# Attention and MLP on one core: q, k, v cast on GpSimd and turned by DMA, A@V in one burst per quad

## The chip, the cores and the metric

The kernel runs on one core of a Trainium2 chip. The metric is device time in microseconds of one execution. Two runs of the kernel before took 523.96 and 526.88 us, median 525.42.

## What is computed

q, k and v are f32 of shape (8, 12, 448, 64): 8 batches, 12 heads, 448 tokens, head size 64. The attention has a squared relu in place of the softmax, and an MLP with prelu follows:

```python
scores = scale * np.matmul(q, k.transpose(0, 1, 3, 2))      # scale = 1/sqrt(64)
attn = np.maximum(scores, 0.0) ** 2 / S                     # S = 448
attn_out = np.matmul(attn, v)
x = attn_out.transpose(0, 2, 1, 3).reshape(B * S, H * D)    # 3584 x 768
h = x @ w_in                                                # 768 x 2048
g = np.maximum(h, 0.0) + alpha * np.minimum(h, 0.0)
out = g @ w_out                                             # 2048 x 768, f32
```

## The kernel before

Four heads make a quad, so a batch has three quads and the program 24. The 448 tokens are split as 64 partitions times 7 (PP and NJ), and a chunk (b, g, j) is one seventh of the keys of one quad.

Loads (`load_batch`, lines 67 to 84): q, k and v of a batch come by DMA from the GpSimd (POOL) queue, which casts f32 to bf16 on the way; q and k in pieces of 64 elements, since heads are interleaved in SBUF. The raw tiles have two buffers, one batch each. w_in comes in 16 transfers (line 92), w_out in one (line 106), on the same queue, between the loads of batches 0 and 1.

`transposes` (line 111): 14 transposes on TensorE turn q and k of a quad, seven each into a PSUM tile `tps` from `mm_ps`, the pool of two banks that the MLP uses too; VectorE copies each to SBUF (qT, kT, line 119).

`scores` (line 121): four 64x64 matmuls into a pair of banks `sc` (two pairs), a relu on ScalarE (line 132) or, for j = 2 and 5, on VectorE (line 134), and a square on VectorE (line 136) give `at`. `attnv` (line 139): four matmuls for each j add up in `av`, one pair of banks with one buffer; after j = 6 ScalarE scales it into xT (line 154).

`ffn1` (line 159): six matmuls into a bank of `mm_ps` (`hps`), relu of the negative on ScalarE (`neg`, line 169), prelu on VectorE into gT (line 170), which frees the bank. `ffn2` (line 175): 16 matmuls into a bank of `mm_ps` (`ops`), copied by ScalarE to `osb` (line 184); two output transfers from the SP queue for each 128 rows.

The order is written by hand, and each engine follows it. The attention of batch 0 runs first. Then batch b's MLP steps (16 of ffn1 with cost 1.12, 6 or 8 of ffn2 with cost 2.6) are mixed with bursts of batch b + 1: a burst is the scores of two chunks and A@V of the two chunks before. A quad's transposes come right after the burst that has chunk j = 2 of the quad ahead of it.

Of the kernel before, what the change touches and what calls it, by code (L numbers as in the profile page):

```python
# [19 lines left out]
PP = 64  # L20
NJ = 7
# [3 lines left out]
def kernel(  # L25
# [32 lines left out]
    ident = singles.tile([128, 128], BF16)  # L58
# [6 lines left out]
    raw = {}  # L65

    def load_batch(b, which, parts):
        src = {"q": q, "k": k, "v": v}[which]
        t = raw.get((b, which))
        if t is None:  # L70
            shape = [128, H // 2, NJ, D] if which == "v" else [128, NG, NJ, 2, D]
            t = raw_pool.tile(shape, BF16, tag=which, name=f"{which}raw")
            raw[(b, which)] = t
        if which == "v":
            flat = src[b].rearrange("(m two) (pp j) d -> (two pp) m (j d)", two=2, j=NJ)
            for lo, hi in parts:
                nc.gpsimd.dma_start(out=t[:, 2 * lo:2 * hi].rearrange("p m j d -> p m (j d)"),  # L77
                                    in_=flat[:, 2 * lo:2 * hi])
        else:
            flat = src[b].rearrange("(m two) (pp j) d -> (two pp) m j d", two=2, j=NJ)  # L80
            for lo, hi in parts:
                for g in range(lo, hi):
                    for s in range(2):
                        nc.gpsimd.dma_start(out=t[:, g, :, s], in_=flat[:, 2 * g + s])  # L84

# [8 lines left out]

    nc.sync.dma_start(out=alpha_sb, in_=moe_alpha.rearrange("(kf p) -> p kf", p=128))
    nc.vector.tensor_scalar(beta_sb, alpha_sb, -1.0, 1.0, ALU.mult, ALU.add)
    make_identity(nc, ident)
    for w in "qkv":
        load_batch(0, w, [(0, 1)])
    for w in "qkv":  # L100
        load_batch(0, w, [(1, 3)])
    for i in range(4):
        load_w_in(512 * i, 512 * i + 512)
    for w in "qkv":
        load_batch(1, w, [(0, 3)])
    nc.gpsimd.dma_start(out=w_out_sb, in_=w_out_v)


    qT, kT, att, av, xT = {}, {}, {}, {}, {}

    def transposes(b, g):
        for name, store, eng in (("q", qT, nc.vector), ("k", kT, nc.vector)):
            ps = mm_ps.tile([128, NJ, 128], BF16, tag="mm", name="tps")
            src = raw[(b, name)]
            for j in range(NJ):
                nc.tensor.transpose(ps[:, j], src[:, g, j].rearrange("p s d -> p (s d)"), ident)  # L116
            dst = qkT_pool.tile([128, 2, NJ, PP], BF16, tag=name, name=f"{name}T")
            store[(b, g)] = dst
            eng.tensor_copy(dst, ps.rearrange("p j (h c) -> p h j c", h=2))  # L119

    def scores(b, g, j):
        ps = sc_ps.tile([128, 2, 512], F32, tag="sc", name="sc")
        qt, kt = qT[(b, g)], kT[(b, g)]
        for r in range(2):
            for c in range(2):
                nc.tensor.matmul(ps[64 * c:64 * c + 64, r, :S],  # L126
                                 kt[64 * r:64 * r + 64, c, j, :],
                                 qt[64 * r:64 * r + 64, c],
                                 start=True, stop=True)
        rl = at_pool.tile([128, 2, S], BF16, tag="rl", name="rl")  # L130
        if j not in (2, 5):
            nc.scalar.activation(rl, ps[:, :, :S], ACTF.Relu)  # L132
        else:
            nc.vector.tensor_scalar(rl, ps[:, :, :S], 0.0, None, ALU.max)  # L134
        a = at_pool.tile([128, 2, S], BF16, tag="at", name="at")
        nc.vector.tensor_tensor(a, rl, rl, ALU.mult)  # L136
        att[(b, g, j)] = a

    def attnv(b, g, j):
        if j == 0:  # L140
            av[(b, g)] = av_ps.tile([128, 2, 512], F32, tag="av", name="av")
        ps = av[(b, g)]
        a = att.pop((b, g, j))
        vv = raw[(b, "v")]
        for r in range(2):
            for s in range(2):
                nc.tensor.matmul(ps[64 * s:64 * s + 64, r, :S],  # L147
                                 vv[64 * r:64 * r + 64, 2 * g + s, j, :],
                                 a[64 * r:64 * r + 64, s],
                                 start=(j == 0), stop=(j == NJ - 1))  # L150
        if j == NJ - 1:
            if g == 0:
                xT[b] = xT_pool.tile([128, NG, 2, S], BF16, tag="xT", name="xT")
            nc.scalar.activation(xT[b][:, g], ps[:, :, :S], ACTF.Copy, scale=out_scale)  # L154


    gT = {}

# [13 lines left out]

    o_sb = {}
# [27 lines left out]

    bursts = {b: [] for b in range(B)}
    pend = []
    for i in range(0, len(chunks), 2):
        new = chunks[i:i + 2]
        bursts[new[0][0]].append((new, pend))
        pend = new
    last_pend = pend

    def emit_burst(new, old):  # L210
        for ch in new:
            scores(*ch)
            if ch[2] == 2:
                n = quads.index(ch[:2]) + 1
                if n < len(quads):
                    todo.append(quads[n])
        for ch in old:
            attnv(*ch)

    todo = []  # L220
    transposes(0, 0)
    for new, old in bursts[0]:
        emit_burst(new, old)
        while todo:
            transposes(*todo.pop(0))
    for b in range(B):
        steps = mlp_steps(b)
        work = bursts[b + 1] if b + 1 < B else []
        total = sum(c for c, _ in steps) * 0.88
        done, n = 0.0, 0  # L230
        if b + 2 < B:
            for w in "qkv":
                load_batch(b + 2, w, [(0, 3)])
        if b == B - 1:
            for ch in last_pend:
                attnv(*ch)
        for cost, fn in steps:
            while n < len(work) and done >= total * n / len(work):
                emit_burst(*work[n])
                n += 1  # L240
                while todo:
                    transposes(*todo.pop(0))
            fn()
            done += cost
        assert n == len(work)

# [29 lines left out]
```

## Time and profile before

| | us |
|---|---|
| median of the two runs | 525.42 |
| profiled execution | 527.37 |
| its span, first to last instruction | 525.6 |
| TensorE busy | 434.0 |
| VectorE busy | 262.0 |
| ScalarE busy | 216.7 |
| GpSimd busy | 112.8 |

The mean granted TensorE clock is 0.936 of full speed. In the tables of waits a row says which line of which engine sat idle until what; in the timeline the bracket at a row's end is the idle time ahead of the row and what ended it. Engines: PE is TensorE, DVE is VectorE, ACT is ScalarE, POOL is GpSimd, SP only issues DMAs. Most of POOL's busy time is the issuing of DMAs.

### The profile page before, as it was taken

Reading aid. Unit: us, or ns where it says so; the run is one execution under the profiler, and the core shown is the slowest. Engines: PE = TensorE matmul, PEld = TensorE weight load, DVE = VectorE, ACT = ScalarE, POOL = GpSimd, SP = SyncE. Lnnn points to the kernel's source line nnn. Section 1 sums busy time; section 2 is a strip of 40 time slices with the busy share of each in tenths; the row PEclk is TensorE's granted clock in tenths of the full one; section 3 lists DMA queues with packets and bytes.
Section 4 is the critical chain, followed back from the end, with each engine's and each line's share of the span. In section 5 each row is a group of like instructions: output and inputs, shape, how many; then the busy total and the mean of one; then the engine's idle time right before and its main releaser. Section 6 shows DMA issues by size and latency. Waiting matters only on the chain.

```text
span 525.6 us, 7922 instructions
## 1 busy us (share of the span) xinstructions
PE 434.0 (83%) x3344; PEld 220.5 (42%) x3344; DVE 262.0 (50%) x393; ACT 216.7 (41%) x329; POOL 112.8 (21%) x128
## 2 busy tenths in 40 slices
PE   2744979888899898898798897897888978989996
PEld 1411434443355443443345443453434533444453
DVE  1855475445653376435755365544655257633500
ACT  1443344443552363353444354534544345343411
POOL 9688066000440008000080004300000000000000
PEclk9775798998999898998999998999989999899998
DMA  9999999160492509423092325914001210012013
GB/s 93 166 187 157 205 141 113 34 110 1 30 106 58 87 0 86 53 62 52 1 104 62 77 38 38 84 46 82 2 1 30 61 31 2 0 31 61 0 43 79
DMA packets 105811, 34.34 MB, mean 65 GB/s; under 512 B 90928, under 2 KB 102192, under 8 KB 105776
## 3 DMA queue, kind: packets, MB, share of 16 engines
q0 software_dynamic: 99232, 22.81, 47.5%
q1 hardware_dynamic: 6544, 11.02, 8.5%
q8 instruction: 26, 0.43, 0.3%
q14 instruction: 9, 0.07, 0.0%
HBM read 45.62 MB, written 11.01 MB: 108 GB/s over the span
## 4 chain that ended last, share of the span: by engine, by line
PE 54%; DVE 20%; ACT 12%; POOL 5%; DMA 5%; issue 4%; ACTq 0%; POOLq 0%
PE ops L178 29%; PE hps L164 20%; DVE at L136 8%; ACT rl L132 7%; DVE rl L134 5%; DVE gT L170 5%; ACT neg L169 4%; DMA vraw<-in_v_dram 3%; PE sc L126 2%; POOL qraw L84 2%; POOL kraw L84 2%; PE av L147 2%; DVE qT L119 2%; DMA w_in_sb<-in_moe_w_in_dram 1%; ACT xT L154 1%
## 5 line engine op out<-in xcount | busy, mean ns | idle before, releaser
L164 PE MATMUL hps<-xT,w_in_sb 128*128 128x448 bf16 x768 | 175.4, 381 | 34.7 <-DVE qT L119 19.9
L178 PE MATMUL ops<-w_out_sb,gT 128*128 128x384 bf16 x896 | 151.5, 326 | 8.5 <-DVE qT L119 6.7
L136 DVE TENSOR_TENSOR at<-rl 128x896 bf16<-128x896 bf16 x168 | 102.6, 624 | 108.1 <-ACT rl L132 103.6
L170 DVE SCALAR_TENSOR_TENSOR gT<-neg,beta_sb,hps 128x448 bf16<-128x448 f32 x128 | 85.6, 678 | 95.6 <-ACT neg L169 95.6
L164 PEld LDWEIGHTS <-w_in_sb 128*128 128x128 bf16 x768 | 77.8, 104 | 127.0 <-issue 75.8
L169 ACT ACTIVATE neg<-hps 128x448 f32<-128x448 f32 x128 | 69.3, 544 | 145.1 <-PE hps L164 145.1
L132 ACT ACTIVATE rl<-sc 128x896 bf16<-128x896 f32 x120 | 106.4, 919 | 31.5 <-PE sc L126 29.7
L178 PEld LDWEIGHTS <-gT 128*128 128x128 bf16 x896 | 85.8, 98 | 72.1 <-issue 18.3
L184 ACT COPY osb<-ops 128x384 f32<-128x384 f32 x56 | 26.8, 478 | 127.0 <-PE ops L178 127.0
L84 POOL DMA_DIRECT2D qraw<-in_q_dram x48 | 46.9, 979 | 103.7 <-PE tps L116 102.7
L147 PE MATMUL av<-at,vraw 64*64 64x448 bf16 x672 | 52.0, 368 | 20.2 <-ACT xT L154 16.7
L134 DVE TENSOR_SCALAR rl<-sc 128x896 bf16<-128x896 f32 x48 | 52.1, 1085 | 14.3 <-PE sc L126 14.3
L126 PE MATMUL sc<-qT,kT 64*64 64x448 bf16 x672 | 52.6, 382 | 4.8 <-ACT rl L132 3.0
L84 POOL DMA_DIRECT2D kraw<-in_k_dram x48 | 46.8, 977 | 15.8 <-DMA w_out_sb<-in_moe_w_out_dram 13.4
L147 PEld LDWEIGHTS <-vraw 64*64 64x64 bf16 x672 | 22.4, 110 | 38.3 <-issue 23.7
L77 POOL DMA_DIRECT2D vraw<-in_v_dram x9 | 7.4, 818 | 119.4 <-PE av L147 119.4
L126 PEld LDWEIGHTS <-kT 64*64 64x64 bf16 x672 | 14.4, 108 | 35.7 <-issue 34.2
L116 PE MATMUL tps<-ident,qraw 128*128 128x128 bf16 x168 | 15.3, 239 | 12.1 <-DMA qraw<-in_q_dram 12.1
L154 ACT ACTIVATE xT<-av 128x896 bf16<-128x896 f32 x24 | 22.3, 929 | 0.0
L116 PE MATMUL tps<-ident,kraw 128*128 128x128 bf16 x168 | 15.2, 238 | 6.1 <-DMA kraw<-in_k_dram 6.1
L119 DVE COPY qT<-tps 128x896 bf16<-128x896 bf16 x24 | 14.8, 618 | 9.8 <-PE tps L116 9.8
L116 PEld LDWEIGHTS <-qraw 128*128 128x128 bf16 x168 | 10.8, 106 | 19.1 <-issue 13.2
(12 smaller groups left out, 41.0 us busy)
## 6 DMA issues: line engine op xcount, KB each, us to landing
out_dram<-osb SPq DMA_DIRECT2D x56, 192.0 KB, 2.7
qraw<-in_q_dram POOLq DMA_DIRECT2D x48, 112.0 KB, 4.1
kraw<-in_k_dram POOLq DMA_DIRECT2D x48, 112.0 KB, 4.4
vraw<-in_v_dram POOLq DMA_DIRECT2D x7, 672.0 KB, 7.4
w_in_sb<-in_moe_w_in_dram POOLq DMA_DIRECT2D x16, 192.0 KB, 7.7
w_out_sb<-in_moe_w_out_dram POOLq DMA_DIRECT2D x1, 3072.0 KB, 23.3
vraw<-in_v_dram POOLq DMA_DIRECT2D x1, 448.0 KB, 7.4
vraw<-in_v_dram POOLq DMA_DIRECT2D x1, 224.0 KB, 5.6
```

Of the source, the lines that this page charges most:

```text
L84: nc.gpsimd.dma_start(out=t[:, g, :, s], in_=flat[:, 2 * g + s])
L116: nc.tensor.transpose(ps[:, j], src[:, g, j].rearrange("p s d -> p (s d)"), ident)
L126: nc.tensor.matmul(ps[64 * c:64 * c + 64, r, :S], kt[64 * r:64 * r + 64, c, j, :], qt[64 * r:64 * r + 64, c], start=True, stop=True)
L132: nc.scalar.activation(rl, ps[:, :, :S], ACTF.Relu)
L134: nc.vector.tensor_scalar(rl, ps[:, :, :S], 0.0, None, ALU.max)
L136: nc.vector.tensor_tensor(a, rl, rl, ALU.mult)
L147: nc.tensor.matmul(ps[64 * s:64 * s + 64, r, :S], vv[64 * r:64 * r + 64, 2 * g + s, j, :], a[64 * r:64 * r + 64, s], start=(j == 0), stop= ...
L154: nc.scalar.activation(xT[b][:, g], ps[:, :, :S], ACTF.Copy, scale=out_scale)
L164: nc.tensor.matmul(ps, w_in_sb[:, km // 2, km % 2, bass.ts(ff, 128)], xT[b][:, km // 2, km % 2, :], start=(km == 0), stop=(km == KM - 1))
L169: nc.scalar.activation(neg, ps, ACTF.Relu, scale=-1.0)
L170: nc.vector.scalar_tensor_tensor(gT[b // 2][:, ff, (b % 2) * S:(b % 2) * S + S], neg, beta_sb[:, ff:ff + 1], ps, ALU.mult, ALU.add)
L178: nc.tensor.matmul(ps, gT[sb][:, ff, bass.ts(c, 128)], w_out_sb[:, ff, bass.ts(hf, 384)], start=(ff == 0), stop=(ff == KF - 1))
```

## The change

Loads: each quad's q, k and v come as plain f32 transfers from the SP queue, one each, with three raw buffers (a quad each), four quads ahead. Three casts then make bf16 tiles, on GpSimd (for quads 0 to 2: k on ScalarE, q on VectorE, v on GpSimd). q and k are turned by one DMA transpose each (SBUF to SBUF, 7 blocks of 128x128) from the SP queue, straight into qT and kT; TensorE's transposes, the identity and the copies on VectorE are gone.

Attention: `attnv` runs a quad's 28 matmuls in one go, in a pair of banks taken from the score pool, after the first scores of the next quad. The pool `av` is gone and `mm_ps` has four banks. All relus are ScalarE's except j = 2 and 5 of quads 0 to 2. The output copy `osb` moves from ScalarE to VectorE. A quad is four bursts (1 + A@V, 2, 2, 2 scores), spread over the MLP steps of the batch before.

Start: the loads of quads 0 to 3 go out on SP, w_in and w_out on POOL ahead of all casts.

```diff
-    sc_ps = ctx.enter_context(tc.tile_pool(name="scps", bufs=2, space=bass.MemoryType.PSUM))
-    av_ps = ctx.enter_context(tc.tile_pool(name="avps", bufs=1, space=bass.MemoryType.PSUM))
-    mm_ps = ctx.enter_context(tc.tile_pool(name="mmps", bufs=2, space=bass.MemoryType.PSUM))
+    sc_ps = pool("scps", 2, **PSUM)
+    mm_ps = pool("mmps", 4, **PSUM)
...
+    def load(n, names="qkv"):
+        b, g = quads[n]
+        for w in names:
+            t = raw_pool.tile([128, 2, NJ, D], F32, tag=w, name=f"{w}raw")
+            raw[(n, w)] = t
+            flat = src[w][b, 4 * g:4 * g + 4].rearrange("(s hf) (pp j) d -> (hf pp) s (j d)", hf=2, j=NJ)
+            nc.sync.dma_start(out=t.rearrange("p s j d -> p s (j d)"), in_=flat)
...
+    def transpose(n, w):
+        store = qT if w == "q" else kT
+        t = cast.pop((n, w))
+        dst = qkT_pool.tile([128, NJ, 2, PP], BF16, tag=w, name=f"{w}T")
+        store[n] = dst
+        nc.sync.dma_start_transpose(out=dst.rearrange("p j h c -> p j (h c)"),
+                                    in_=t.rearrange("p j s d -> p (j s d)"))
...
+    def attnv(n):
+        b, g = quads[n]
+        ps = sc_ps.tile([128, 2, 512], F32, tag="sc", name="av")
+        for j in range(NJ):
+            a = att.pop((n, j))
...
-        nc.scalar.copy(o[:, bass.ts(hf, 384)], ps)
+        nc.vector.tensor_copy(o[:, bass.ts(hf, 384)], ps)
...
+    relu_on_dve = {(n, j) for n in range(NG) for j in (2, 5)}
...
+        if i == 0:
+            if n < NQ:
+                scores(n, 0)
+            if n > 0:
+                attnv(n - 1)
+        elif n < NQ:
+            scores(n, 2 * i - 1)
+            scores(n, 2 * i)
+
+        if i == 0 and n + 4 < NQ:
+            load(n + 4)
+        if i == 1 and n + 1 < NQ and n > 0:
+            transpose(n + 1, "k")
+            transpose(n + 1, "q")
+        if i == 2 and n + 2 < NQ and n > 0:
+            for w in "kqv":
+                to_bf16(n + 2, w, nc.gpsimd)
...
+    for n in range(3):
+        if n < 3:
+            to_bf16(n, "k", nc.scalar)
+            to_bf16(n, "q", nc.vector)
+            to_bf16(n, "v", nc.gpsimd)
+        if n < 2:
+            transpose(n, "k")
+            transpose(n, "q")
```

VectorE's queue in the middle of the program, among the MLP steps of a batch. Before, with the relus of line 134, the squares of line 136 and the copies of line 119:

```order
L134 TENSOR_SCALAR rl<-sc 128x896
L136 TENSOR_TENSOR at<-rl 128x896 x2
L119 COPY qT<-tps 128x896
L119 COPY kT<-tps 128x896
L170 SCALAR_TENSOR_TENSOR gT<-neg,beta_sb,hps 128x448 x3
```

The changed kernel at such a place (L134 is now the square, L166 the prelu, L178 the output copy):

```order
L166 SCALAR_TENSOR_TENSOR gT<-neg,beta_sb,hps 128x448 x2
L134 TENSOR_TENSOR at<-rl 128x896
L166 SCALAR_TENSOR_TENSOR gT<-neg,beta_sb,hps 128x448 x3
L134 TENSOR_TENSOR at<-rl 128x896 x2
L178 COPY osb<-ops 128x384
```

The relus and the copies of qT and kT have left this queue, and the output copy has come. SP's queue at the start of the changed kernel, at the loads of quad 3, with what each row waits for (DMAHW: an earlier transfer's landing; Activation, DVE, Pool: a cast on that engine); before, SP had only alpha and the output transfers:

```order
L81 DMA kraw<-in_k_dram 128x2x448 [waits DMAHW2_49,Activation_49]
L81 DMA qraw<-in_q_dram 128x2x448 [waits DMAHW3_49,DVE_49]
L81 DMA vraw<-in_v_dram 128x2x448 [waits DMAHW4_49,Pool_49]
L105 DMA_TRANSPOSE kT<-kb 128x7x128 [waits DMAHW5_49]
L105 DMA_TRANSPOSE qT<-qb 128x7x128 [waits DMAHW6_49]
L105 DMA_TRANSPOSE kT<-kb 128x7x128 [waits DMAHW7_49,Activation_49]
```

These are the loads of quad 3 and the transposes of quads 0 and 1; the v load of quad 3 reuses the buffer of quad 0's v and waits for its cast on POOL. The start of POOL's queue, before:

```order
L84 DMA qraw<-in_q_dram 128x7x64 x4
L84 DMA kraw<-in_k_dram 128x7x64 x4
L77 DMA vraw<-in_v_dram 128x4x448
L92 DMA w_in_sb<-in_moe_w_in_dram 64x3x512 x16
L84 DMA qraw<-in_q_dram 128x7x64 x6
```

and in the changed kernel:

```order
L114 DMA w_in_sb<-in_moe_w_in_dram 64x3x512 x16
L224 DMA w_out_sb<-in_moe_w_out_dram 128x16x768
L87 CAST vb<-vraw 128x896 x3
L87 CAST kb<-kraw 128x2x7x64
L87 CAST qb<-qraw 128x2x7x64
```

The weights are now first, and the cast of quad 0's v stands behind all of them.

## Rows read from the trace of the kernel before

**Rows 1.** The page, busy time, share of the span and instructions of TensorE.
```profile
PE 434.0 (83%) x3344; PEld 220.5 (42%) x3344; DVE 262.0 (50%) x393; ACT 216.7 (41%) x329; POOL 112.8 (21%) x128
```
**Rows 2.** Waits of the whole span: who waited for whom, us, times, longest.
```profile
PE hps L164 <- DVE qT L119: 19.9, 13, 2.2
...
PE av L147 <- ACT xT L154: 16.7, 12, 1.6
```
**Rows 3.** One period by windows: all, line 116 alone, line 164 alone.
```profile
237.60:360.70 123.10, 105.95 (x837) 53.67 (x837) 65.16 (x98) 53.57 (x83) 25.01 (x26) 0.96 0.53 57
...
237.60:360.70 123.10, 5.99 (x84) 4.78 (x84) 0.96 0.53 57
...
237.60:360.70 123.10, 44.08 (x193) 19.40 (x193) 0.96 0.53 57
```
**Rows 4.** Waits of TensorE in that period.
```profile
PE hps L164 <- DVE qT L119: 5.9, 4, 2.2
PE av L147 <- ACT xT L154: 4.6, 3, 1.6
PE hps L164 <- DVE gT L170: 2.9, 6, 1.1
PE ops L178 <- DVE qT L119: 2.2, 2, 1.5
PE hps L164 <- ACT xT L154: 1.3, 1, 1.3
```
**Rows 5.** Timeline of TensorE: start, us, operation, idle before and releaser.
```profile
242.99 5.18 PE L164 MATMUL hps<-xT,w_in_sb 128*128 128x448 bf16 x18 [2.18 <-DVE qT L119]
...
248.50 0.55 PE L147 MATMUL av<-at,vraw 64*64 64x448 bf16 x8
248.98 2.44 PE L164 MATMUL hps<-xT,w_in_sb 128*128 128x448 bf16 x12
...
260.86 0.38 PE L147 MATMUL av<-at,vraw 64*64 64x448 bf16 x4 [1.56 <-ACT xT L154]
```
**Rows 6.** A window behind that wait; third from the end is the clock.
```profile
244.00:247.00 3.00, 3.00 (x11) 1.27 (x10) 0.68 (x1) 0.54 (x1) 0.00 (x0) 0.62 0.00 0
```
**Rows 7.** Groups by line in the period: busy us, mean ns, idle before.
```profile
L132 ACT ACTIVATE rl<-sc 128x896 bf16<-128x896 f32 x30 | 26.6, 920 | 0.1
L136 DVE TENSOR_TENSOR at<-rl 128x896 bf16<-128x896 bf16 x42 | 25.7, 624 | 30.9 <-ACT rl L132 29.6
...
L170 DVE SCALAR_TENSOR_TENSOR gT<-neg,beta_sb,hps 128x448 bf16<-128x448 f32 x32 | 21.4, 678 | 22.7 <-ACT neg L169 22.7
...
L134 DVE TENSOR_SCALAR rl<-sc 128x896 bf16<-128x896 f32 x12 | 13.0, 1085 | 4.4 <-PE sc L126 4.4
...
L184 ACT COPY osb<-ops 128x384 f32<-128x384 f32 x14 | 6.7, 478 | 32.3 <-PE ops L178 32.3
...
L119 DVE COPY qT<-tps 128x896 bf16<-128x896 bf16 x6 | 3.7, 617 | 0.0
```
**Rows 8.** Timeline: w_in's eighth and ninth, and two first MLP matmuls.
```profile
21.69 1.24 POOL L92 DMA_DIRECT2D w_in_sb<-in_moe_w_in_dram  x2 [2.58 <-DMA vraw<-in_v_dram]
...
54.65 5.48 PE L164 MATMUL hps<-xT,w_in_sb 128*128 128x448 bf16 x18
...
478.06 0.93 PE L164 MATMUL hps<-xT,w_in_sb 128*128 128x448 bf16 x4
```
**Rows 9.** A GpSimd row; hardware queue (packets, MB, share); DMA issues (KB, us to landing).
```profile
masks.py:199 POOL TENSOR_SCALAR_AFFINE_SELECT ident<-ident 128x128 bf16<-128x128 bf16 x1 | 0.3, 287 | 0.1
...
q1 hardware_dynamic: 6544, 11.02, 8.5%
...
out_dram<-osb SPq DMA_DIRECT2D x56, 192.0 KB, 2.7
...
kraw<-in_k_dram POOLq DMA_DIRECT2D x48, 112.0 KB, 4.4
```
**Rows 10.** A window in which w_out arrives; the last column is GB/s.
```profile
52.00:56.00 4.00, 3.52 (x22) 2.21 (x23) 1.49 (x3) 0.00 (x0) 0.98 (x1) 0.50 1.14 207
```

More of the change, by code (lines that the diff above doesn't have):

```diff
@@ L8 @@
 from concourse._compat import with_exitstack
-from concourse.masks import make_identity
 F32 = mybir.dt.float32
@@ L62 @@
     beta_sb = singles.tile([128, KF], F32)
[L65 to L78, printed above, removed]
-        else:
[L80 to L84, printed above, removed]
+    quads = [(b, g) for b in range(B) for g in range(NG)]
@@ new lines, with copy @@
+    raw, cast, qT, kT, vb = {}, {}, {}, {}, {}
+    src = {"q": q, "k": k, "v": v}
+    def load(n, names="qkv"):
[5 more added lines that the diff above has]
+            nc.sync.dma_start(out=t.rearrange("p s j d -> p s (j d)"), in_=flat)
+    def copy(eng, o, i):
+        if eng is nc.scalar:
+            nc.scalar.copy(o, i)
+        else:
+            eng.tensor_copy(o, i)
@@ new lines, in to_bf16 @@
+    def to_bf16(n, w, eng):
+        r = raw.pop((n, w))
+        if w == "v":
+            t = v_pool.tile([128, 2, NJ, D], BF16, tag="v", name="vb")
+            vb[n] = t
+            copy(eng, t, r)
+        else:
+            t = cast_pool.tile([128, NJ, 2, D], BF16, tag=w, name=f"{w}b")
+            cast[(n, w)] = t
+            copy(eng, t.rearrange("p j s d -> p s j d"), r)
+    def transpose(n, w):
[5 more added lines that the diff above has]
+                                    in_=t.rearrange("p j s d -> p (j s d)"))
@@ L93, in load_w_in, with scores @@
                                     in_=w_in_v[hf, e, :, :, lo:hi])
[L95 to L121, printed above, removed]
+    att, xT = {}, {}
+    def scores(n, j):
         ps = sc_ps.tile([128, 2, 512], F32, tag="sc", name="sc")
-        qt, kt = qT[(b, g)], kT[(b, g)]
         for r in range(2):
@@ L126, in scores @@
                 nc.tensor.matmul(ps[64 * c:64 * c + 64, r, :S],
[L127 to L128 removed]
+                                 kT[n][64 * r:64 * r + 64, j, c, :],
+                                 qT[n][64 * r:64 * r + 64, :, c, :],
                                  start=True, stop=True)
[L130 to L131 removed]
+        rl = rl_pool.tile([128, 2, S], BF16, tag="rl", name="rl")
@@ L132, in scores @@
+        if (n, j) in relu_on_dve:
+            nc.vector.tensor_scalar(rl, ps[:, :, :S], 0.0, None, ALU.max)
+        else:
             nc.scalar.activation(rl, ps[:, :, :S], ACTF.Relu)
-        else:
-            nc.vector.tensor_scalar(rl, ps[:, :, :S], 0.0, None, ALU.max)
         a = at_pool.tile([128, 2, S], BF16, tag="at", name="at")
         nc.vector.tensor_tensor(a, rl, rl, ALU.mult)
[L137 to L154, printed above, removed]
@@ L157 @@
-    gT = {}
+        att[(n, j)] = a
+    def attnv(n):
[3 more added lines that the diff above has]
+            a = att.pop((n, j))
+            for r in range(2):
+                for s in range(2):
+                    nc.tensor.matmul(ps[64 * s:64 * s + 64, r, :S],
+                                     vb[n][64 * r:64 * r + 64, s, j, :],
+                                     a[64 * r:64 * r + 64, s],
+                                     start=(j == 0), stop=(j == NJ - 1))
+        if g == 0:
+            xT[b] = xT_pool.tile([128, NG, 2, S], BF16, tag="xT", name="xT")
+        nc.scalar.activation(xT[b][:, g], ps[:, :, :S], ACTF.Copy, scale=out_scale)
@@ L159, in ffn1 @@
+    gT, o_sb = {}, {}
     def ffn1(b, ff):
@@ L200, in mlp_steps @@
         return steps
[L202 to L225, printed above, removed]
+    NQ = len(quads)
+    relu_on_dve = {(n, j) for n in range(NG) for j in (2, 5)}
+    def burst(n, i):
+        if i == 0:
[14 more added lines that the diff above has]
+                to_bf16(n + 2, w, nc.gpsimd)
@@ new lines @@
+    for w in "kq":
+        load(0, w)
+    load(0, "v")
+    nc.scalar.dma_start(out=alpha_sb, in_=moe_alpha.rearrange("(kf p) -> p kf", p=128))
+    for n in (1, 2, 3):
+        load(n, "kqv")
+    for i in range(4):
+        load_w_in(512 * i, 512 * i + 512)
+    nc.gpsimd.dma_start(out=w_out_sb, in_=w_out_v)
+    nc.vector.tensor_scalar(beta_sb, alpha_sb, -1.0, 1.0, ALU.mult, ALU.add)
+    for n in range(3):
[6 more added lines that the diff above has]
+            transpose(n, "q")
+        if n == 0:
+            continue
+        for i in range(4):
+            burst(n - 1, i)
@@ L226 @@
+    for i in range(4):
+        burst(2, i)
+    work = [(n, i) for n in range(NG, NQ) for i in range(4)] + [(NQ, 0)]
+    w = 0
     for b in range(B):
         steps = mlp_steps(b)
-        work = bursts[b + 1] if b + 1 < B else []
-        total = sum(c for c, _ in steps) * 0.88
-        done, n = 0.0, 0
[L231 to L236, printed above, removed]
+        if b + 1 < B:
+            mine = work[w:w + 12] if w else work[:12]
+        else:
+            mine = []
+        w += len(mine)
+        if b == 0:
+            pass
+        total = sum(c for c, _ in steps) * 0.95
+        done, n = 0.0, 0
+        burst(*((b + 1) * NG, 0)) if b + 1 == B else None
@@ L237 @@
         for cost, fn in steps:
-            while n < len(work) and done >= total * n / len(work):
-                emit_burst(*work[n])
+            while n < len(mine) and done >= total * n / len(mine):
+                burst(*mine[n])
                 n += 1
-                while todo:
-                    transposes(*todo.pop(0))
             fn()
             done += cost
-        assert n == len(work)
+        assert n == len(mine)
 _INS = ['q', 'k', 'v', 'moe_w_in', 'moe_w_out', 'moe_alpha']
```

26 lines of the change are left out of this document (14 added, 12 removed).

## The prediction

> **What bounds the kernel now.** I read the page's busy times first [rows 1]: TensorE works 434.0 of 525.6 us, so what it waits for is what can be won. The table of waits [rows 2] names the two largest: the first matmuls of an MLP step wait 19.9 us in all for VectorE's copy of a transposed q, and A@V waits 16.7 us for the copy of its only accumulator to xT.
>
> In the middle the program repeats every two batches, and I read one such period, 237.6 to 360.7 us [rows 3]: 123.1 us, TensorE busy 105.95, clock 0.96. Its idle time by releaser [rows 4] is 5.9 + 4.6 + 2.9 + 2.2 + 1.3 = 16.9 us; the 2.9 are waits for gT, the prelu that frees one of the MLP's two banks. The timeline [rows 5] shows one quad's turn: behind the transposes 2.18 us of waiting for VectorE, because transposes and MLP share two banks, then 18 MLP matmuls in 5.18 us, where 12 take 2.44 elsewhere (3.66 for 18). A window behind that wait [rows 6] says why: the granted clock is 0.62 there, so part of the time at the lower level, 1.2 GHz. One wait of 2.18 us thus costs 1.5 us more. Over the period the 32 MLP steps of line 164 take 44.1 us [rows 3]; at 1.22 each they would take 39.0, so 5.1 us go to the clock.
>
> **The change, part by part, for one period (six quads).**
>
> *Transposes leave TensorE*: line 116 takes 6.0 us [rows 3]. Saved: 6.0.
>
> *Waits*: no transpose asks for an MLP bank (5.9 + 2.2 gone), A@V takes a bank pair whose last reader, a relu, was issued two or three MLP steps earlier (4.6 gone), and with four banks TensorE can run four steps of 1.22 us ahead of gT (2.9 gone). The wait for xT stays: at each batch's start the 28 A@V matmuls stand directly ahead of the matmuls that read their result. That is 1.3 us [rows 4], now twice a period: 2.6 left. Saved: 16.9 - 2.6 = 14.3. What must cover this is ACT and DVE. By the period's rows [rows 7] ACT now does 30 relus (26.6); it gets 42, 12 more at 0.92 = 11.0, and gives away the 14 output copies (6.7): 53.6 [rows 3] + 11.0 - 6.7 = 57.9 us. DVE loses its 12 relus (13.0) and the copies of q and k (3.7, and as much again), and gets the 14 copies, which I price at ACT's 6.7: 65.2 - 20.4 + 6.7 = 51.5 us. Both stay well under TensorE's time.
>
> *Clock*: with no stall of two microseconds left I take the 5.1 us as saved; 0 is the other end.
>
> *A@V in one burst*: eight A@V matmuls take 0.55 us, four of them 0.38 [rows 5], so each further group of four costs about 0.18 and the end of a group 0.2 once. 28 in a row take 1.5 us; seven bursts' worth now pay that end 3.5 times. About 0.2 per quad is exposed: 1.0.
>
> Sum: 6.0 + 14.3 + 5.1 + 1.0 = 26.4 per period, so 96.7 us instead of 123.1, or 13.2 a batch. Seven batches run between the first MLP matmul (54.65) and the last batch's (478.06) [rows 8]: 92 us. The last batch runs almost alone before and after; I leave it as it is.
>
> *Casts on GpSimd*: 18 a period. The trace has no cast there. From below, VectorE's copy of a tile of that size, 0.62 us [rows 7]; from above GpSimd's only compute row, 287 ns for 128 elements a partition [rows 9], times seven = 2.0. So 11 to 36 us of 96 on an engine that has nothing else to do after the start: cost 0, because each cast stands three bursts ahead of its transpose, some 12 us; the second rival is what it costs if that cover is gone.
>
> *DMA transposes*: 48 of 224 KB, behind each other and the loads in SP's queue. The trace has none. Lower bound: SP's output transfer of 192 KB lands in 2.7 us [rows 9]. Upper: k comes in 112 KB transfers of 64-element pieces that land in 4.4 us [rows 9]; two of them, 8.8 us. I take 3.0, since the size and the queue are those of the output transfer. Per quad SP's queue then holds three loads of 448 KB (1.1 us at w_out's rate, below; 1.9 at the 246 GB/s that 11.02 MB in 8.5% of 525.6 us make [rows 9]), 2.3 outputs of 0.8 us and two transposes: 5.2 to 7.5, middle 6.3, + 6.0 = 12.3 us, and TensorE needs 96.7 / 6 = 16.1. Hidden, cost 0. The Trainium skill ("VectorE: DVE Perf Modes", The three transpose paths) speaks against this part: one 128x128 bf16 block costs 390 ns on TensorE and 1309 ns through the DMA crossbar; seven blocks in series would be an estimated 9.2 us, a little over the upper bound, and the sum would be that of the first rival. No row here shows it.
>
> *The start*: here the change costs. Weights now go first on POOL, and SP's fourth v load waits for a GpSimd cast that stands behind all 16 w_in transfers and w_out (the last fence of order); the transposes of quad 0 stand behind that load. POOL lets only eight transfers be open (here w_in's eighth waited 2.58 us for the v load eight places ahead of it [rows 8]), so w_in's ninth waits for its first. w_out moved 207 GB/s of bf16, so about 415 GB/s of f32 read [rows 10]. The queue puts loads 0 to 6 (21 x 0.459 = 9.6 MB) ahead of the transpose of quad 3, which TensorE needs before the first MLP step, and the weights (12.6 MB of f32) run beside them: 22.2 MB, 53 us. With landing, eight transposes and the scores behind the last I take 65 us for the first MLP matmul instead of 54.65: +10. If the weights did not compete, loads 0 to 3 and w_in alone (11.8 MB, 28 us) and three quads of about 6 us give 46; if each step waits for the one before, 85.
>
> *Allowance* for late casts and A@V operands: +8, between 0 and the second rival's 27.
>
> Against the profiled execution's own 527.37 us (525.6 of span): 527.4 - 92 + 10 + 8 = **453 us**; the median of the runs, 525.42, is 2 us below that execution. The forecast's own range is 430 to 473.
>
> **Rivals.**
>
> 1. *The DMA transposes become the bound (slower).* At T us each, a quad takes 2T + 6.3 in SP's queue. Above T = 4.9 this exceeds TensorE's 16.1, and scores wait for kT and qT. Over 21 quads, with eight more at the start, the loss is 21 (2T - 9.8) + 8 (T - 3), and it eats the 74 us of gain at T = 6.1. At 8.8: 164 + 46 more, about 660 us. For it: the loads in small pieces [rows 9] show what many short packets cost. Against: SP's large transfers. Chance 0.12 above 6.1, and 0.06 for 4.9 to 6.1, 470 to 525 us.
>
> 2. *Casts hold VectorE.* Among the MLP's first steps a quad comes with 9.5 steps: TensorE 9.5 x 1.22 + 2.9 = 14.5 us, DVE 9.5 x 0.678 + 7 x 0.624 = 10.8 [rows 7]. If each square waits out a cast of 2.0 us, three a quad, DVE needs 16.8, 2.3 too many, for 1.7 quads a batch, 7 batches: 27 us, so 453 - 8 + 27 = 472. No row has VectorE and GpSimd computing together. Chance 0.12. The skill's "SBUF — State Buffer" (Who interferes with whom) says that a VectorE instruction with two SBUF inputs and a GpSimd one that reads SBUF exclude each other for their whole length; the square is of that kind. By that rule this rival is the mechanism, and how often they meet decides; no row here shows it.
>
> 3. *The start is later still*, 85 us: 473. Chance 0.07.
>
> **How the numbers follow.** The forecast has 0.62, the rivals 0.12 + 0.06, 0.12 and 0.07; 0.01 is left for anything else. Faster by over 2% (under 515, about what a measurement of this kernel can tell from no change): forecast, rivals 2 and 3 and part of rival 1, 0.84. Within 2%: 0.04. Slower: 0.12. The range takes in the later start, the casts and a part of the middling transposes, and leaves out the slow ones: 428 to 500.
>
> **What would show it.** Right: no wait of hps for a DVE copy, TensorE's clock near 1.0 from 80 us on, periods of 95 to 99 us, transposes landing in 3 to 5 us behind the loads, SP idle between quads. Wrong: sc waiting for DMA kT or qT each quad (rival 1); squares of over 0.62 us or idle DVE beside POOL's casts, and hps waiting for gT (rival 2); a first hps after 75 us (rival 3); or a DVE or ACT over 65 us a period.

## The result, and the profile after

Two runs of the changed kernel took 457.07 and 457.84 us, median 457.45, against 525.42 before: ratio 0.871, 95% interval 0.860 to 0.882. The forecast was 453 in a range of 428 to 500, "faster" with 0.84. The time came out 4 us above the forecast, but two of the forecast's terms were wrong by more than that, and they lie on opposite sides. The profiled execution took 457.07 us, its span 455.3.

Busy times and share of the span, from the page (before: [rows 1]):

```profile
PE 387.0 (85%) x3008; PEld 191.2 (42%) x3008; DVE 233.6 (51%) x362; ACT 229.3 (50%) x318; POOL 76.4 (17%) x87
```

One period of two batches, by windows (columns: window, its length, busy time of TensorE, weight load, VectorE, ScalarE and GpSimd, TensorE's clock, DMA share, GB/s; the share is the packets' time over that of 16 DMA engines and can pass 1), all instructions and then line 160 alone, which is the MLP's first step and has TensorE's columns only (before: [rows 3]). Under them TensorE's waits in the same window, of which there is only one kind (before: [rows 4]):

```profile
127.40:222.20 94.80, 94.47 (x753) 46.40 (x753) 56.61 (x88) 57.33 (x80) 17.34 (x19) 1.00 0.60 147
...
127.40:222.20 94.80, 38.90 (x193) 17.71 (x193) 1.00 0.60 147
...
PE hps L160 <- ACT xT L150: 0.5, 3, 0.2
```

TensorE is busy for 94.47 of 94.80 us and its clock is 1.00. No bank, no transpose and no VectorE copy holds it any more; the middle of the program is now bound by TensorE's own work.

Groups of VectorE and GpSimd in that window (before: [rows 7]):

```profile
L134 DVE TENSOR_TENSOR at<-rl 128x896 bf16<-128x896 bf16 x42 | 28.3, 677 | 13.5 <-ACT rl L132 12.3
...
L178 DVE COPY osb<-ops 128x384 f32<-128x384 f32 x14 | 7.8, 558 | 13.7 <-PE ops L172 13.2 <-DMA out_dram<-osb 0.5
L87 POOL CAST vb<-vraw 128x896 bf16<-128x896 f32 x7 | 7.3, 1046 | 46.3 <-PE av L144 46.3
...
L87 POOL CAST kb<-kraw 128x896 bf16<-128x896 f32 x6 | 5.6, 935 | 31.7 <-DMA kT<-kb 31.7
```

VectorE and ScalarE work 57 us each of 95, and a cast takes 0.94 to 1.05 us.

Where batches begin their MLP, from TensorE's timeline, first of the changed kernel (batches 0, 1 and 7) and then batch 1 of the one before, whose batches 0 and 7 are in [rows 8]:

```profile
80.56 4.88 PE L160 MATMUL hps<-xT,w_in_sb 128*128 128x448 bf16 x18
...
126.33 0.93 PE L160 MATMUL hps<-xT,w_in_sb 128*128 128x448 bf16 x4
127.42 2.81 PE L160 MATMUL hps<-xT,w_in_sb 128*128 128x448 bf16 x14 [0.16 <-ACT xT L150]
...
410.46 0.93 PE L160 MATMUL hps<-xT,w_in_sb 128*128 128x448 bf16 x4
```

```profile
110.31 0.93 PE L164 MATMUL hps<-xT,w_in_sb 128*128 128x448 bf16 x4
```

That splits the whole difference in three. Start: the first MLP matmul comes at 80.56 instead of 54.65, 25.9 us later. Seven batches: 410.46 - 80.56 = 329.9 us instead of 478.06 - 54.65 = 423.4, 93.5 less. Rest: 457.07 - 410.46 = 46.6 us instead of 527.37 - 478.06 = 49.3, 2.7 less. 527.37 + 25.9 - 93.5 - 2.7 = 457.1. So the seven batches did what the forecast said (92), and the start cost 16 us more than the 10 that it gave.

What the start waits for: TensorE's waits over the whole span, and SP's queue with the transposes of quads 0 and 1 (start, time that the issue held the queue).

```profile
PE sc L124 <- DMA qT<-qb: 51.8, 2, 49.2
PE sc L124 <- ACT rl L132: 8.5, 12, 1.0
```

```profile
27.31 1.32 SPq L105 DMA_TRANSPOSE kT<-kb  x1
28.69 6.97 SPq L105 DMA_TRANSPOSE qT<-qb  x1
35.75 3.08 SPq L105 DMA_TRANSPOSE kT<-kb  x1
38.93 12.30 SPq L105 DMA_TRANSPOSE qT<-qb  x1
```

TensorE has no score matmul before 49.2 us. The chain of work that ended last (start, us, what) has the reason: POOL issues w_out at 24.75, casts v of quad 0, SP issues quad 3's v load and two transposes, and the second of them takes 20.47 us to land.

```profile
28.69 20.47 DMA qT<-qb
```

In the middle of the program the same instruction is a small thing: the twelve of the period above hold SP's queue for 1.2 to 3.7 us, 2.0 in the mean. The DMA issues over the whole span (KB, median us from issue to landing):

```profile
w_out_sb<-in_moe_w_out_dram POOLq DMA_DIRECT2D x1, 3072.0 KB, 29.7
kT<-kb SPq DMA_TRANSPOSE x24, 5.6
qT<-qb SPq DMA_TRANSPOSE x24, 4.8
```

w_out, 29.7 us from issue to landing, is under way while the four slow transposes hold the queue.

### The profile page after: what moved, and what is told of

It reads as the page before. It is cut to its first block, busy times and chain, and to the rows that moved or that the text cites. A ratio compares the mean times of both kernels' runs of the same rounds, so it can differ in the third digit from the quotient of the medians.

```text
span 455.3 us, 7491 instructions
## 1 busy us (share of the span) xinstructions
PE 387.0 (85%) x3008; PEld 191.2 (42%) x3008; DVE 233.6 (51%) x362; ACT 229.3 (50%) x318; POOL 76.4 (17%) x87
## 2 busy tenths in 40 slices
DMA packets 76097, 61.82 MB, mean 136 GB/s; under 512 B 48928, under 2 KB 72480, under 8 KB 76064
## 3 DMA queue, kind: packets, MB, share of 16 engines
q10 hardware_dynamic: 2064, 0.01, 0.3%
## 4 chain that ended last, share of the span: by engine, by line
PE 82%; DMA 11%; ACT 3%; issue 1%; POOL 0%; SPq 0%; DVE 0%; ACTq 0%; POOLq 0%
PE ops L172 33%; PE hps L160 32%; PE sc L124 9%; PE av L144 8%; DMA qT<-qb 6%; DMA w_in_sb<-in_moe_w_in_dram 5%; ACT rl L132 2%; ACT xT L150 1%; SPq L105 0%; DVE at L134 0%; POOL w_out_sb L224 0%; POOL vb L87 0%; DVE osb L178 0%; SPq L81 0%; ACTq L132 0%
## 5 line engine op out<-in xcount | busy, mean ns | idle before, releaser
L132 ACT ACTIVATE rl<-sc 128x896 bf16<-128x896 f32 x162 | 141.4, 916 | 127.1 <-PE sc L124 125.0
L134 DVE TENSOR_TENSOR at<-rl 128x896 bf16<-128x896 bf16 x168 | 111.3, 667 | 89.9 <-ACT rl L132 84.7
L160 PE MATMUL hps<-xT,w_in_sb 128*128 128x448 bf16 x768 | 155.9, 355 | 1.1 <-ACT xT L150 1.1
L166 DVE SCALAR_TENSOR_TENSOR gT<-neg,beta_sb,hps 128x448 bf16<-128x448 f32 x128 | 86.1, 677 | 51.6 <-ACT neg L165 50.4
L165 ACT ACTIVATE neg<-hps 128x448 f32<-128x448 f32 x128 | 70.3, 549 | 47.3 <-PE hps L160 46.1
L178 DVE COPY osb<-ops 128x384 f32<-128x384 f32 x56 | 31.2, 558 | 60.3 <-PE ops L172 59.4
L87 POOL CAST vb<-vraw 128x896 bf16<-128x896 f32 x24 | 24.4, 1023 | 153.3 <-PE av L144 139.8
L87 POOL CAST kb<-kraw 128x896 bf16<-128x896 f32 x21 | 20.2, 960 | 119.6 <-DMA kT<-kb 98.0
L144 PE MATMUL av<-at,vb 64*64 64x448 bf16 x672 | 39.9, 377 | 0.0
L144 PEld LDWEIGHTS <-vb 64*64 64x64 bf16 x672 | 21.7, 114 | 12.0 <-issue 1.5
L87 POOL CAST qb<-qraw 128x896 bf16<-128x896 f32 x21 | 21.5, 1025 | 3.3 <-DMA qT<-qb 3.0
L114 POOL DMA_DIRECT2D w_in_sb<-in_moe_w_in_dram x16 | 10.1, 634 | 13.1 <-DMA w_in_sb<-in_moe_w_in_dram 12.3
L130 DVE TENSOR_SCALAR rl<-sc 128x896 bf16<-128x896 f32 x6 | 6.5, 1082 | 0.0
## 6 DMA issues: line engine op xcount, KB each, us to landing
w_out_sb<-in_moe_w_out_dram POOLq DMA_DIRECT2D x1, 3072.0 KB, 29.7
```

The source lines that it names most:

```text
L87: eng.tensor_copy(o, i)
L114: nc.gpsimd.dma_start(out=w_in_sb[64 * hf:64 * hf + 64, :, e, lo:hi], in_=w_in_v[hf, e, :, :, lo:hi])
L144: nc.tensor.matmul(ps[64 * s:64 * s + 64, r, :S], vb[n][64 * r:64 * r + 64, s, j, :], a[64 * r:64 * r + 64, s], start=(j == 0), stop=(j == ...
L160: nc.tensor.matmul(ps, w_in_sb[:, km // 2, km % 2, bass.ts(ff, 128)], xT[b][:, km // 2, km % 2, :], start=(km == 0), stop=(km == KM - 1))
L165: nc.scalar.activation(neg, ps, ACTF.Relu, scale=-1.0)
L166: nc.vector.scalar_tensor_tensor(gT[b // 2][:, ff, (b % 2) * S:(b % 2) * S + S], neg, beta_sb[:, ff:ff + 1], ps, ALU.mult, ALU.add)
```

## Experiments

Every edit below is against the changed kernel (457.45 us). A ratio is to the kernel before on the same chip.

**1. w_out later.** Is it w_out that makes the first transposes slow?

```diff
-    nc.gpsimd.dma_start(out=w_out_sb, in_=w_out_v)
     nc.vector.tensor_scalar(beta_sb, alpha_sb, -1.0, 1.0, ALU.mult, ALU.add)
...
     for i in range(4):
         burst(2, i)
+    nc.gpsimd.dma_start(out=w_out_sb, in_=w_out_v)
```

> The transfer of w_out moves behind the attention of batch 0 in GpSimd's queue; nothing else changes. Theory A: in the changed kernel the first four DMA transposes (the one of quad 0's q took 20.5 us from issue to landing) were slow because w_out was arriving beside them in their many small pieces. Then that transpose lands in under 9 us, the first scores start near 37 us instead of 49.2, the first MLP matmul near 67 instead of 80.6, and the kernel takes about 444 us. Theory B: the transposes stood behind the loads ahead of them in SP's queue, or are slow by themselves: the first scores stay at 46 to 50 us and the time at 454 to 460.

448.5 us, ratio 0.854 (0.851 to 0.858). Piece of the chain, and TensorE's first scores and first MLP step:

```profile
28.42 9.62 DMA qT<-qb
...
38.09 0.61 PE sc L124 x4
```

```profile
70.24 4.36 PE L160 MATMUL hps<-xT,w_in_sb 128*128 128x448 bf16 x18
```

q of quad 0 lands in 9.6 us instead of 20.5, the first scores come 11.1 us earlier and the first MLP step 10.3. So about half of that landing was w_out's doing; the other half remains beside the loads and the last w_in transfers. The total gains only 9.0 us, nearer to theory A than to B but short of A's 444: w_out now meets the transposes of a later quad. The landing of that quad's q, whose transpose held SP's queue for 9.9 us, and TensorE waiting for it:

```profile
66.73 19.79 DMA qT<-qb
```

```profile
86.66 0.38 PE L124 MATMUL sc<-qT,kT 64*64 64x448 bf16 x4 [2.29 <-DMA qT<-qb]
```

The collision moves with w_out. That is the strongest sign for the cause: the slowest transpose is the one beside this transfer, 20.5 us to land at the start and 19.8 here. In the changed kernel the transposes issued at 35.75 and 38.93 had only w_out and one another beside them from 36 us on, and landed in 19.1 and 16.8.

**2. v of quads 0 to 2 cast on VectorE.** Is it SP's wait for POOL's cast (the fence on SP's start in the part on the change) that delays the transposes?

```diff
-            to_bf16(n, "v", nc.gpsimd)
+            to_bf16(n, "v", nc.vector)
```

> The casts of v of quads 0 to 2 move from GpSimd to VectorE, so that SP's v load of quad 3 no longer waits for a cast behind all weight transfers. Theory C: this wait (SP stood from 14 to 26.9 us) is what makes the start late: the first transpose is issued near 16 us instead of 27.3, the first scores start 10 us earlier, the time is about 447. Theory A: the transposes meet the weights' transfers anyway, now w_in and then w_out; the first scores gain 5 us at most and the time is 452 to 458.

456.3 us, ratio 0.869 (0.866 to 0.873). The wait is gone and nothing is won:

```profile
17.55 10.85 SPq L105 DMA_TRANSPOSE kT<-kb  x1
...
48.66 0.96 PE L124 MATMUL sc<-qT,kT 64*64 64x448 bf16 x8 [48.66 <-DMA qT<-qb]
```

k's transpose is issued 9.8 us earlier, holds the queue for 10.85 us instead of 1.32, and q's lands when it did. The semaphore in the queue named one culprit, and the full DMA engines behind it were the other, which binds.

**3. Both edits together.**

> The two edits before together. If both waits are real and add up, the first scores start near 26 us, the first MLP matmul near 57, and the time is about 434 us. If one hides the other, it is that of the better one alone, about 444.

448.5 us (446.9 to 450.2), ratio 0.854 (0.850 to 0.859), the same as with w_out alone. SP's first transpose, and TensorE's first scores:

```profile
17.01 10.85 SPq L105 DMA_TRANSPOSE kT<-kb  x1
```

```profile
37.50 0.96 PE L124 MATMUL sc<-qT,kT 64*64 64x448 bf16 x8 [37.50 <-DMA qT<-qb]
```

w_out is not the only transfer that slows a transpose: it is issued at 59.4 here, and k's first transpose, 10 us earlier than in the changed kernel, takes 19.7 us to land beside w_in and the loads. Even with both edits the first scores are not before 37.5 us, while the kernel before has its transposes of k done at 11 us. As long as the first transposes go by DMA beside the loads and weights, the start stays late.

**4. The start's transposes on TensorE.** Quads 0 to 4 are turned on TensorE through a bank of the MLP's pool, as before; all later ones by DMA. The transposes of quads 2 and 3 stand one burst later in the order, those of quad 1 within quad 0's attention, the start's casts of k and q stand two bursts ahead of their quad instead of in a block, v of quads 0 to 2 is cast on VectorE, and w_out comes after the attention of quad 1.

```diff
+        if n < 5:
+            ps = mm_ps.tile([128, NJ, 128], BF16, tag="mm", name="tps")
+            for j in range(NJ):
+                nc.tensor.transpose(ps[:, j], t[:, j].rearrange("p s d -> p (s d)"), ident)
+            nc.vector.tensor_copy(dst.rearrange("p j h c -> p j (h c)"), ps)
+            return
...
-        if i == 1 and n + 1 < NQ and n > 0:
+        if i == 2 - (n > 2) and n + 1 < NQ and n > 0:
...
+            if i == 3:
+                to_bf16(n, "v", nc.vector)
+            burst(n, i)
...
+        if n == 1:
+            nc.gpsimd.dma_start(out=w_out_sb, in_=w_out_v)
```

> Quads 0 to 4 are transposed on TensorE as in the kernel before (into the MLP's banks, copies on VectorE), v of quads 0 to 2 is cast on VectorE, w_out is issued after the attention of quad 1; from quad 5 on all is as in the changed kernel. Theory: the late start is only the DMA transposes' path. Then the first scores start near 10 us, the first MLP matmul at 33 to 42, and the steady periods stay at 94.8 us: 410 to 420 us. Rival: the start is bound by the loads and weights themselves (11.8 MB of f32 that the first MLP step needs, 28 us at 415 GB/s, more with what is loaded ahead), so the first MLP matmul comes no earlier than 50 and the time is 428 or more.

425.5 us, ratio 0.810 (0.808 to 0.813), between the theory and its rival. The first scores come at 14.5 us, the first MLP step at 49.30, which is later than hoped:

```profile
49.30 2.04 PE L169 MATMUL hps<-xT,w_in_sb 128*128 128x448 bf16 x5
```

Two of the chain's first pieces are a part of the reason:

```profile
0.74 11.38 DMA alpha_sb<-in_moe_alpha_dram
...
12.31 0.54 DVE qb L90
```

VectorE's first instruction computes beta from alpha, 8 KB (2,064 packets, by the page's row of its queue) that need 11.4 us to arrive beside the loads; the cast of q stands behind it. Experiment 5 moves that instruction. The time lies 32 us under the changed kernel's: 31.3 from the start (80.56 to 49.30).

**5. That start with less on VectorE.** As 4, but beta is computed after the attention of batch 0, ScalarE copies kT of quads 0 to 2, and v of quads 1 and 2 is cast on GpSimd.

```diff
-    nc.vector.tensor_scalar(beta_sb, alpha_sb, -1.0, 1.0, ALU.mult, ALU.add)
...
+            copy(nc.scalar if w == "k" and n < 3 else nc.vector, dst.rearrange("p j h c -> p j (h c)"), ps)
...
+            if i == (0 if n else 3):
+                to_bf16(n, "v", nc.gpsimd if n else nc.vector)
...
+    nc.vector.tensor_scalar(beta_sb, alpha_sb, -1.0, 1.0, ALU.mult, ALU.add)
```

> The kernel with TensorE's transposes for the first five quads, with three more moves at the start: the small operation on alpha, for which VectorE's queue waited until 12 us, is issued after the attention of batch 0; kT's copy of quads 0 to 2 goes to ScalarE; v of quads 1 and 2 is cast on GpSimd. Theory: VectorE is what the attention of batch 0 waits for (it is busy 3.7 to 4.0 of every 4 us there). Then the first scores start near 10 us instead of 14.5, the first MLP matmul at 38 to 43 instead of 49.3, and the time is 413 to 420. Rival: the loads set the pace (281 GB/s until 36 us): the first MLP matmul at 47 or later and 422 or more.

420.3 us (419.4 to 420.5), ratio 0.799 (0.797 to 0.802): the fastest here, 37 us under the changed kernel and 105 under the one before, and just above the theory's 413 to 420. First scores, first MLP step, and one period by windows:

```profile
8.45 0.96 PE L133 MATMUL sc<-qT,kT 64*64 64x448 bf16 x8 [0.72 <-DVE qT L90]
...
43.94 4.27 PE L169 MATMUL hps<-xT,w_in_sb 128*128 128x448 bf16 x17
```

```profile
90.07:184.84 94.77, 94.46 (x757) 46.39 (x753) 56.34 (x89) 57.33 (x80) 18.52 (x18) 1.00 0.55 146
```

The period is that of the changed kernel; the whole gain is the start, 80.56 - 43.94 = 36.6 us. From the first scores to the first MLP step it still takes 35.5 us (31.4 in the changed kernel). In that stretch TensorE waits 9.9 us for ScalarE's relus, its own transposes take 5.4, and its clock is 0.74; no DMA transpose lies in it, and what would shorten it was not tried.

**6. Two banks for the MLP instead of four.** How much of the steady gain are the banks?

```diff
-    mm_ps = pool("mmps", 4, **PSUM)
+    mm_ps = pool("mmps", 2, **PSUM)
```

> The MLP's PSUM pool gets two banks instead of four (two banks of PSUM stay unused); nothing else changes. Theory: the four banks do real work, since ScalarE now has all relus: behind each pair of scores the MLP step's relu waits up to 1.8 us for two relus, and with two banks TensorE stands until VectorE's gT frees one, about 1 us a burst, six or seven bursts a batch. The time is 480 to 505 us, and the waits name hps on gT. Rival: with the transposes gone from that pool two banks are enough: 457 to 463.

477.8 us, ratio 0.909 (0.906 to 0.912): 20 us slower, a little under the theory's range and far from the rival's. TensorE's waits over the whole span, and one period:

```profile
PE hps L160 <- DVE gT L166: 12.6, 31, 0.9
...
PE ops L172 <- DVE gT L166: 2.1, 4, 0.6
```

```profile
128.30:228.56 100.26, 95.79 (x756) 46.41 (x752) 55.59 (x89) 57.33 (x80) 17.82 (x18) 1.00 0.53 139
```

The period is 5.5 us longer; the seven batches take 17.8 us more than in the changed kernel and the last one 3.0. 14.7 of these 20.8 are waits for the prelu that frees a bank, each 0.9 at most: with two banks TensorE can no longer run ahead of VectorE while a burst of scores occupies it. The clock stays at 1.00 here, so stalls of this length did not lower it; behind a wait of 2.2 us it was 0.62 before [rows 5, 6].

**7. All transposes back on TensorE,** in the four-bank pool, with VectorE's copies; the rest as changed. What are the DMA transposes worth?

```diff
-        nc.sync.dma_start_transpose(out=dst.rearrange("p j h c -> p j (h c)"),
-                                    in_=t.rearrange("p j s d -> p (j s d)"))
+        ps = mm_ps.tile([128, NJ, 128], BF16, tag="mm", name="tps")
+        for j in range(NJ):
+            nc.tensor.transpose(ps[:, j], t[:, j].rearrange("p s d -> p (s d)"), ident)
+        nc.vector.tensor_copy(dst.rearrange("p j h c -> p j (h c)"), ps)
```

> The DMA transposes of all quads are undone: q and k are turned on TensorE into the MLP's pool, now of four banks, with copies on VectorE, at the same places of the order; loads, casts and the rest stay. Theory: the period of two batches grows from 94.8 by the 6.0 us that line 116 took before and little more, since four banks cover the copies: 101 to 104 us; the start gains 20 to 28 us, so in all 452 to 464. Rival: the MLP waits for the copies again as before (8.1 us a period and the clock behind it): periods of 108 us or more, 475 or more.

452.3 us, ratio 0.860 (0.857 to 0.864): 5 us *faster* than the changed kernel, about 1%; the ends of the two ratio intervals overlap, but the stages below add up to it. The first MLP step, one period and its squares:

```profile
51.70 4.21 PE L165 MATMUL hps<-xT,w_in_sb 128*128 128x448 bf16 x18
```

```profile
100.04:202.45 102.41, 99.69 (x840) 51.14 (x837) 67.55 (x101) 57.74 (x80) 19.49 (x18) 1.00 0.35 109
```

```profile
L139 DVE TENSOR_TENSOR at<-rl 128x896 bf16<-128x896 bf16 x43 | 33.8, 798 | 11.9 <-ACT rl L137 10.6
```

In the middle the DMA transposes win 102.4 - 94.8 = 7.6 us in this period and 23.5 us over the seven batches (353.4 here, 329.9 in the changed kernel). At the start they lose more: here the first MLP step is at 51.70 instead of 80.56, 28.9 us earlier, though w_out and the casts are where they were. As built, the DMA transposes gave the kernel nothing; the other parts (banks, A@V from the score banks, the moved relus and copies) carry 525 to 452.

**8. Each DMA transpose from quad 3 on issued twice.** Are they near to binding?

```diff
+        if n >= 3:
+            again = twice_pool.tile([128, NJ, 2, PP], BF16, tag="tw", name="again")
+            nc.sync.dma_start_transpose(out=again.rearrange("p j h c -> p j (h c)"),
+                                        in_=t.rearrange("p j s d -> p (j s d)"))
```

> From quad 3 on each DMA transpose is issued twice, the second into a tile that nobody reads, so SP's queue holds four transposes a quad. With my price of 3.0 us of the queue each, a quad needs 6.3 + 12 = 18.3 us there against TensorE's 15.8, and the time is about 505 us, with scores that wait for the transposes. If a transpose holds the queue for under 2 us, the copies stay hidden and the time is 457 to 468.

456.8 us, ratio 0.869 (0.866 to 0.872): no loss at all. SP's queue for one quad, and the landing of q's extra ones:

```profile
163.47 1.33 SPq L106 DMA_TRANSPOSE kT<-kb  x1
164.85 1.28 SPq L110 DMA_TRANSPOSE again<-kb  x1
166.19 1.86 SPq L106 DMA_TRANSPOSE qT<-qb  x1
168.09 1.30 SPq L110 DMA_TRANSPOSE again<-qb  x1
```

```profile
again<-qb SPq DMA_TRANSPOSE x21, 2.8
```

The four transposes of this quad hold the queue for 5.8 us, those of the six quads of a period 7.3 in the mean and 9.1 at most, of 15.8 us a quad. By the first rival two of them had to hold 9.8 us to bind, so it is refuted even at twice their number.

**9. The casts from quad 3 on on VectorE.** Do GpSimd's casts slow VectorE's squares, and does it cost time?

```diff
-                to_bf16(n + 2, w, nc.gpsimd)
+                to_bf16(n + 2, w, nc.vector)
```

> From the third quad on, the casts of q, k and v to bf16 run on VectorE instead of GpSimd; all else as in the changed kernel. Theory (GpSimd's casts stretch VectorE's squares, and the stretch lies off the path): the squares' mean goes from 667 ns back to about 625, VectorE gains some 18 casts of 0.62 us a period less the 1 or 2 us that the squares no longer lose, so about 65 us of each 94.8, and the time stays at 455 to 459 us. Rival (GpSimd's casts cost path time): under 452 us. Other rival (VectorE with the casts becomes late for the score copies): over 462 us.

461.0 us (460.2 to 461.8), ratio 0.878 (0.874 to 0.881).

```profile
L134 DVE TENSOR_TENSOR at<-rl 128x896 bf16<-128x896 bf16 x168 | 103.5, 624 | 81.0 <-ACT rl L132 77.6
```

```profile
127.00:222.00 95.00, 93.76 (x750) 45.98 (x739) 62.74 (x106) 57.35 (x80) 0.00 (x0) 1.00 0.60 146
```

The squares are back at exactly the 624 ns of [rows 7], from 667 over the whole span of the changed kernel: the stretch is GpSimd's. VectorE works 62.7 us of 95. The time is some 3 us worse, a little above the theory's 455 to 459; TensorE's waits for gT (2.8 us in all) and for a relu of quad 2 (1.1) name most of that. The two intervals of the ratio overlap, so the difference is not firm. That the casts on GpSimd cost path time is refuted.

## Why the prediction came out where it did

**The seven batches: right, 92 against 93.5.** Transposes: line 116's 6.0 us a period are gone. Clock: line 160 takes 38.90 us where line 164 took 44.08 [rows 3], 5.2 saved against 5.1 foreseen; the granted clock is 1.00 all through. Waits: of the 2.6 us of xT waits that I kept, 0.5 is left. The row at 127.42 shows why: the first four matmuls of a batch's MLP read the two older quads of xT, their 0.93 us cover ScalarE's copy, and only 0.16 is seen; I had carried the 1.3 over from [rows 4], where the copy started later. So a period is 94.8, not 96.7. That this did not make the saving larger is a second small error on the other side: I multiplied 13.2 by seven, but batch 0's MLP ran 110.31 - 54.65 = 55.7 us before and 45.8 after, 9.9 saved only. Three periods of about 27.9 (83.6 together) and 9.9 make 93.5.

Two smaller terms were off. A@V in one burst was priced too low by its own line, 12.10 us a period before and 8.96 after where I gave 1.0; but TensorE's busy time fell by 11.5 in all, only 0.3 more than transposes and clock. My 51.5 us for VectorE came out at 56.6: the squares and the output copies take 2.6 and 1.1 more, and I subtracted groups that overlap (before, they add up to 67.5 in 65.2 busy).

How the gain divides: experiment 6 puts 20 us on the banks, experiment 7 23.5 us on taking the transposes off TensorE. Each was undone alone and not both at once, so how far the two overlap is open.

**The start: wrong, 10 foreseen, 25.9 measured.** The step that failed is the overlap that the sum took for granted, and in it the price of the first transposes. First, I let loads and weights stream for 53 us at 415 GB/s of f32 read, with the attention of batch 0 under them, and put "landing, eight transposes and the scores behind the last" into the 12 us up to 65. The stream came near that rate. By queue (packets, MB, share of the 16 DMA engines' time; q0 has the weights, counted in bf16 as in [rows 10], q1 what SP issues), from 12 to 28 us and from 36 to 52:

```profile
q0 software_dynamic: 1707, 1.61, 59.5%
q1 hardware_dynamic: 1710, 2.88, 54.8%
```

```profile
q0 software_dynamic: 1810, 2.78, 94.7%
q1 hardware_dynamic: 1811, 0.45, 21.7%
```

The DMA engines are full in both. In the first 2 x 1.61 + 2.88 = 6.1 MB are read in 16 us, 381 GB/s; in the second w_out alone reads 5.6 MB, and the transposes move 0.45. But the four transposes held SP's queue from 27.3 to 51.2 us, and the loads of quads 4 to 6, which I had streaming by then, went out only behind them:

```profile
51.29 0.57 SPq L81 DMA_DIRECT2D qraw<-in_q_dram  x1
```

And the attention of batch 0 ran under none of it: it began with the first q at 49.2 us and took 31.4 more.

Second, I priced a transpose by the queue it stands in (3.0 us) and not by the transfers it runs beside. The price was too high in the middle, 2.0 us of queue in the mean, and far too low beside w_out, 20.5 us to land. My upper bound of 8.8 came from the nearest row of short packets [rows 9], but that row was not taken beside a 3 MB transfer. Experiment 1 takes w_out away and gets 11 us of the landing back; experiment 7 takes the transposes off the DMA engines, with nothing else moved, and has the first MLP step 28.9 us earlier; experiment 4, which moves w_out, the casts and the order too, 31.3. The wait of SP for POOL's cast, on which the text spent most words, is true as an order and, by experiment 2, not what binds. The third rival (85 us for the first MLP step) was the nearest to what happened, and I gave it 0.07.

The batch-0 attention behind that is also longer than I reckoned: three quads of 6 us were 31.4 us (49.20 to 80.56), with a clock of 0.72, waits for ScalarE's relus (8.5) and one for the q of quad 2 (2.6):

```profile
49.20:80.60 31.40, 18.79 (x173) 8.25 (x173) 20.41 (x29) 16.91 (x19) 8.18 (x8) 0.72 1.07 258
```

**The allowance of 8: not needed,** no cast and no A@V operand was late in the middle. **The last batch at 0:** 2.7 us were won; its clock is 1.00 instead of 0.97, and its waits for gT and xT went from 1.9 us to 0.2. So 92 + 0 - 10 - 8 = 74 foreseen, 93.5 + 2.7 - 25.9 = 70.3 measured: that the total came out right is in part luck, the allowance standing in for a start that was mis-sized.

**The casts: right in cost, with the mechanism of the second rival seen.** 0.94 to 1.05 us lie between the bounds of 0.62 and 2.0. VectorE and GpSimd at the same moment:

```profile
135.66 2.61 DVE L134 TENSOR_TENSOR at<-rl 128x896 bf16<-128x896 bf16 x2
```

```profile
135.60 0.94 POOL L87 CAST kb<-kraw 128x896 bf16<-128x896 f32 x1 [8.10 <-DMA kT<-kb]
136.74 1.06 POOL L87 CAST qb<-qraw 128x896 bf16<-128x896 f32 x1 [0.21 <-POOL kb L87]
```

Two squares take 2.61 us instead of 1.25 while two casts run. The Trainium skill's "SBUF — State Buffer" (Who interferes with whom) has such a pair exclude each other, and this trace and experiment 9 agree as to the squares: 667 ns in the mean with the casts on GpSimd, 624 without. But 168 x 43 ns is 7 us in all, on an engine that idles 38 of 95; the 27 us of that rival assumed that each of a quad's three casts holds VectorE up for 2.0 us. In experiment 7, with the copies of q and k on VectorE again, the squares averaged 798 ns; no run shows why.

**The transposes as a bound: rightly left as a rival.** The estimate of 9.2 us that I drew from the Trainium skill's "VectorE: DVE Perf Modes" (The three transpose paths) by setting seven blocks in series does not agree with the trace: one instruction with seven blocks holds the queue for 2.0 us in the mean in the middle, and its median landing is 4.8 to 5.6 us behind the loads. **The output copy** was priced at ScalarE's 478 ns and takes VectorE 558, 1.1 us a period on an engine with slack.

What stays open: experiment 1 shows that w_out doubles the landing, and experiment 3 that w_in with the loads can do as much, but neither by which resource (the many short packets of a transpose, some 930 each, since the page counts 48,928 packets under 512 B and experiment 7, without the 48 transposes, 4,384; or turns at the same DMA engines). Plain loads were slowed at the start as well: the five that SP issued from 12 to 28 us landed in 10 to 15 us (medians of q, k and v), against 4.6 to 6.3 over the whole span. No run kept the weights' bytes and changed only their pieces or their queue.

## What to carry to other kernels

Price a DMA transpose by what else the DMA engines carry in that stretch, not by its size: here the same instruction landed in a few microseconds in the middle and in 20 beside the weights. A change that is worth its place in the steady state can lose all of it at the start, so decide by stage: transposes on TensorE while TensorE is idle and the DMA engines are full, by DMA once it is the other way round (420 us against 452 and 457 for one way throughout; of the 32 us to 452, some 8 are the other edits of the start, by the first MLP step at 43.94 instead of 51.70). And when a queue's semaphore seems to hold the path, ask what stands behind it before pricing its removal.

## What the runs showed that was not expected

- A DMA transpose of 128x896 bf16 took from 1.2 us of its queue (landing 2.8 us in the median for the repeated ones of q) to 20.5 us of landing beside a 3 MB weight transfer.
- The 8 KB of alpha took 11.4 us to land beside the first loads (experiment 4), and stood ahead of all of VectorE's work; in the kernel before they took 3.0.
- Waits of up to 0.9 us, 31 of them, left TensorE's granted clock at 1.00 (experiment 6), where a wait of 2.2 us was followed by 0.62 before [rows 5, 6].
